# Holding back the residual transposes of two batches, and one DMA for both attention transposes of a step

## The chip, the cores and the metric

The kernel runs on one core of one Trainium2 chip. The metric is the device time of a whole execution in microseconds (us). Four engines compute on the core: TensorE (PE, with its weight loads shown as PEld), VectorE (DVE), ScalarE (ACT) and GpSimd (POOL). SyncE (SP) computes nothing here; it issues DMAs. POOL issues DMAs too, beside small copies. Sixteen DMA engines move the data of all of them.

## The reference

Eight batches, twelve heads, 448 tokens, head size 64. An attention with a squared ReLU in place of the softmax is followed by an MLP mixer: one pair of products over the tokens, one over the channels, each with a residual.

```python
scores = scale * np.matmul(q, k.transpose(0, 1, 3, 2))
attn = np.maximum(scores, 0.0) ** 2 / S
x = np.matmul(attn, v)            # then [B, S, H * D] = [8, 448, 768]

xt = x.transpose(0, 2, 1)
h = np.maximum(xt @ w_tok1, 0.0) @ w_tok2      # 448 -> 256 -> 448
u = x + h.transpose(0, 2, 1)
h2 = np.maximum(u @ w_ch1, 0.0) @ w_ch2        # 768 -> 1536 -> 768
return u + h2
```

Inputs and output are float32; the loads cast to bfloat16.

## The kernel before

**Tiling.** A step `i` takes four heads of one batch, so a batch has `DB` = 3 steps and the kernel `ND` = 24. In a step, `scores(i, c)` makes the score tiles for seven chunks of 64 keys (PE, L165), ACT applies the ReLU (L174), DVE squares (L181), `values` multiplies by V (PE, L193), and `values_out` writes the scaled result, channels on the partitions, into `xT` (L211). `xT` has one slot for even and one for odd batches, with 512 columns for the 448 tokens and zeros behind them.

**Token mixing.** The first product over the tokens needs the tokens on the partitions. `x_back` makes that transpose into `x_sb`: for the first `XDMA` = 8 steps with PE and a copy (L237, L246), from step index 8 on with DMA transposes issued by SP, one for each of the step's two blocks of 128 channels (L229). `token1` (L255) and `token2` (L278) are the two products; the addition at L286 writes `uT`, the mixed activations with channels on the partitions, for two batches in one tile (`uT_tiles`).

**Channel mixing.** `channel1` (L323) and `channel2` (L362) are the products over the channels. The second gives tokens on the partitions, so its residual must be turned as well: `u_back` issues on SP two DMA transposes a step from `uT` into `u_sb` (L311), six for a batch, 384 columns wide in even batches and 512 in odd ones, so that a pair of batches makes seven chunks of 128 tokens. L369 adds `u_sb` to the product, half a chunk at a time, and after the second half L381 stores the chunk with two DMAs on SP.

**Order.** The schedule is manual: each engine runs its instructions in the order in which the program emits them, and waits are derived from the tiles that they read and write. Loop index `i` from 4 on does `values(i - 1)`, `x_back(i - 1)`, `token1(i - 1)` and `token2(i - 1)`; by the index of the loop, step 7 holds `token2(6)`, step 8 `x_back(7)`, and step 9 `x_back(8)`, the first with DMA transposes. Between them `fill` takes units of channel mixing from `queue`, so that PE always has work; `channel_work(b)` puts a batch's units there, and the `channel2` units of batch 0 wait in `later` until those of batch 1 are queued. `channel2` runs for the first time in step 8.

**When residuals are turned.** `token2` calls `u_back` at once for the first two batches (L294, L295). For the others it leaves the step in `u_later`, which the main loop empties after `x_back` of the next index (L538, L539).

**POOL's queue.** Loads of Q, K and V (`load_four`) and of the weights go through POOL. `load_four(i + PRE)`, three steps ahead, is emitted once in each step; from index 9 on a one-element copy (`gate`, L542) stands before it that reads the last transposed `x_sb`, so that loads start only after it has landed. The last large weight load, the second half of `wc2`, is issued in step 5 (at 65 us).

**Buffers.** `x_sb`, `uT` and `r2` have two slots, `u_sb` and the output tile three, the raw Q, K and V tiles four. PSUM: two slots for scores, one for each of the two accumulators, two for the products (`bank`).

Of the kernel before, what the change touches and what calls it, by code (L numbers as in the profile page):

```python
# [10 lines left out]
BF16 = mybir.dt.bfloat16  # L11
# [5 lines left out]
def kernel(  # L17
# [11 lines left out]
    nc = tc.nc  # L29
# [6 lines left out]
    NP = H // 2  # L36
    ND = B * H // 4
    DB = H // 4
# [6 lines left out]
    NT = 2 * S // 128  # L45
# [7 lines left out]
    mix = ctx.enter_context(tc.tile_pool(name="mix", bufs=2))  # L53
# [8 lines left out]
    xT = [consts.tile([128, NP, SP], BF16, name=f"xT{i}") for i in range(2)]  # L62
# [115 lines left out]
    def square(keep=0):  # L178
        while len(squares) > keep:
            at = squares.pop(0)  # L180
            nc.vector.tensor_tensor(out=at, in0=at, in1=at, op=ALU.mult)  # L181
# [38 lines left out]
    x_tiles, r1_tiles, uT_tiles = {}, {}, {}  # L220
    XDMA = 8

    def x_back(i, place="bank", copy=None):
        b, d = divmod(i, DB)
        x_sb = mix.tile([128, 2, 4, 128], BF16, name="x_sb")
        x_tiles[i] = x_sb
        if i >= XDMA:
            for r in range(2):
                nc.sync.dma_start_transpose(  # L229
                    out=x_sb[:, r], in_=xT[b % 2][:, 2 * d + r, :]  # L230
                )
            return
        pool = ps_mm if place == "bank" else ps_acc
        ps = pool.tile([128, 2, 512], BF16, tag=place, name="x_ps")
        for r in range(2):
            for c in range(4):
                nc.tensor.matmul(  # L237
                    ps[:, r, c * 128 : (c + 1) * 128],
                    lhsT=xT[b % 2][:, 2 * d + r, c * 128 : (c + 1) * 128],
                    rhs=ident,  # L240
                    is_transpose=True,
                    start=True,
                    stop=True,
                    skip_group_check=True,
                )
        (copy or nc.vector.tensor_copy)(  # L246
            x_sb.rearrange("n r c d -> n (r c d)"), ps.rearrange("n r t -> n (r t)")
        )
# [17 lines left out]
    def token2(i, early=False, rs=(0, 1)):  # L266
        b, d = divmod(i, DB)
        if d == 0 and b % 2 == 0 and 0 in rs:
            uT_tiles[b // 2] = mix.tile([128, NP, 2 * S], BF16, name="uT_sb")
        r1 = r1_tiles[i]  # L270
        off = (b % 2) * S
        if early:
            parts = {r: ps_mm.tile([128, 512], FP32, tag="bank", name="h_ps1") for r in rs}
        else:
            parts = {r: ps_acc.tile([128, 512], FP32, tag=f"acc{r}", name="h_ps") for r in rs}
        for r in rs:
            for j in range(JC):
                nc.tensor.matmul(  # L278
                    parts[r][:, :S],
                    lhsT=r1[:, j, r * 128 : (r + 1) * 128],  # L280
                    rhs=wt2[:, j, :],
                    start=(j == 0),
                    stop=(j == JC - 1),
                )
        for r in rs:
            nc.vector.tensor_tensor(  # L286
                out=uT_tiles[b // 2][:, 2 * d + r, off : off + S],
                in0=parts[r][:, :S],
                in1=xT[b % 2][:, 2 * d + r, :S],
                op=ALU.add,  # L290
            )
        if 1 in rs:
            u_later.append(i)
            if i < 2 * DB:  # L294
                u_back(u_later.pop())  # L295


    r2_tiles, u_tiles, out_tiles = {}, {}, {}
    u_later = []

    def chunks(b):
        half = NT // 2
        return range(half) if b % 2 == 0 else range(half, NT)

    def u_back(i):
        b, d = divmod(i, DB)
        t = chunks(b)
        if d == 0:
            u_tiles[b] = mix.tile([128, NP, NT - NT // 2, 128], BF16, name="u_sb", bufs=3)
        for p in (2 * d, 2 * d + 1):  # L310
            nc.sync.dma_start_transpose(  # L311
                out=u_tiles[b][:, p, : len(t), :],
                in_=uT_tiles[b // 2][:, p, t.start * 128 : t.stop * 128],
            )

    def channel1(b, e):
        if b % 2 == 0 and e == 0 and b > 0:
            r2_tiles[b // 2] = mix.tile([128, EC, 2 * S], BF16, name="r2_sb")
        uT, r2 = uT_tiles[b // 2], r2_tiles[b // 2]
        off = (b % 2) * S  # L320
        ps = ps_mm.tile([128, 512], FP32, tag="bank", name="m1_ps")
        for g in range(CC):
            nc.tensor.matmul(  # L323
                ps[:, :S],
                lhsT=wc1[:, g, e * 128 : (e + 1) * 128],
                rhs=uT[:, g, off : off + S],
                start=(g == 0),
                stop=(g == CC - 1),
            )
        nc.scalar.activation(r2[:, e, off : off + S], ps[:, :S], AF.Relu)  # L330
# [23 lines left out]
    def channel2(b, t, half):  # L354
        r2 = r2_tiles[b // 2]
        cols = slice(half * HN, (half + 1) * HN)
        if half == 0:
            out_tiles[b, t] = outp.tile([128, DM], FP32, name="out_sb")
        o = out_tiles[b, t]
        ps = ps_mm.tile([128, 512], FP32, tag="bank", name="m2_ps")  # L360
        for e in range(EC):
            nc.tensor.matmul(  # L362
                ps[:, :HN],
                lhsT=r2[:, e, t * 128 : (t + 1) * 128],
                rhs=wc2[:, e, cols],
                start=(e == 0),
                stop=(e == EC - 1),
            )
        nc.vector.tensor_tensor(  # L369
            out=o[:, cols].rearrange("n (g d) -> n g d", d=128),  # L370
            in0=ps[:, :HN].rearrange("n (g d) -> n g d", d=128),
            in1=u_tiles[b][:, half * (CC // 2) : (half + 1) * (CC // 2), t - chunks(b).start, :],
            op=ALU.add,
        )
        last = b == B - 1 and t == NT - 1
        if half == 1 or last:
            part = cols if last else slice(0, DM)
            (b0, c0), (b1, c1) = divmod(2 * t, QC), divmod(2 * t + 1, QC)
            rows = [out[2 * (b // 2) + n].rearrange("(p c) m -> c p m", c=QC) for n in range(2)]
            for k, (n, c) in enumerate(((b0, c0), (b1, c1))):  # L380
                (nc.scalar if last and k else nc.sync).dma_start(  # L381
                    out=rows[n][c, :, part], in_=o[64 * k : 64 * (k + 1), part]
                )
        if half == 1:
            out_tiles.pop((b, t))
# [5 lines left out]
    def channel_work(b):  # L391
        for e in range(2 if b == 0 else 0, EC):
            queue.append((C1, lambda e=e: channel1(b, e)))
        for t in chunks(b):
            for j in range(2):
                later.append((C2, lambda t=t, j=j: channel2(b, t, j)))
        if b > 0:
            queue.extend(later)
            later.clear()
# [90 lines left out]
    i = DB  # L490
# [31 lines left out]
    for i in range(DB + 1, ND + 2):  # L522
        slow = i <= 2 * DB
        if i == 2 * DB + 1:
            rate[0] = (EC * C1 + NT * C2) / DB
        if i < ND:
            scores(i, 0)
            scores(i, 1)
        if 0 <= i - 1 < ND:
            values(i - 1, range(QC))  # L530
            values_out(i - 1)
        if i < ND:
            scores(i, 2)
        if i - 1 < XDMA:
            fill(1 / 3, least=1)
        if 0 <= i - 1 < ND:
            x_back(i - 1)
        while u_later:  # L538
            u_back(u_later.pop(0))  # L539
        if i + PRE < ND:  # L540
            if i - 1 >= XDMA:
                nc.gpsimd.tensor_copy(gate, x_tiles[i - 1][:1, 1, 3, 127:])  # L542
            load_four(i + PRE)
        if i == 5:
            load_wc2(1, 2)
        square()
        if i - 1 >= XDMA:
            fill(1 / 3)
        if i < ND:
            scores(i, 3)  # L550
            scores(i, 4)
        if i + 1 < ND:
            transposes(i + 1)
        square()
        if not slow:
            fill(2 / 9)
        if 0 <= i - 1 < ND:
            token1(i - 1)
        fill(1 / 3 if slow else 1 / 9, least=1)
        if i < ND:  # L560
            scores(i, 5)
            scores(i, 6)
        if 0 <= i - 1 < ND:
            token2(i - 1)
            if (i - 1) % DB == DB - 1:
                channel_work((i - 1) // DB)
        square()
        fill(1 / 3, least=1 if slow else 0)
    while queue:
# [31 lines left out]
```

## Time and profile before

| | before |
|---|---|
| median of 4 runs | 380.24 us (379.65 to 380.87) |
| the profiled execution | 379.94 us |
| its span in the profile | 378.2 us |
| granted TensorE clock | 1.00 |
| L323, channel1 on PE | 115.6 us busy, x564 |
| L362, channel2 on PE | 115.2 us busy, x672 |
| u_sb transposes (L311, SP) | 48, 3.9 us from issue to landing (median) |
| x_sb transposes (L229, SP) | 32, 2.4 us |
| POOL's gate copy (L542) | 12, 211 ns each |
| software DMA queue (POOL's loads) | 24,416 packets, 21.47 MB, 40.2% of 16 engines |
| hardware DMA queue (SP's) | 45,072 packets, 20.76 MB, 26.1% |

In the profile a group's line names its source line, its engine and operation, and the tiles it writes and reads. Busy time of PE is modelled for pipelined matmuls, so a PE that is always busy is not one at its peak; but a gap in it is time in which it had nothing to start. "X <- Y" under waits means that X stood idle until Y was done. A DMA instruction on SP or POOL is only the issue; the landing is counted from the issue to the arrival of the data. SP's issuing instructions don't count as busy time.

### The profile page before, as it was taken

Reading aid. Unit: us, or ns where it says so; the run is one execution under the profiler, and the core shown is the slowest. Engines: PE = TensorE matmul, PEld = TensorE weight load, DVE = VectorE, ACT = ScalarE, POOL = GpSimd, SP = SyncE. Lnnn points to the kernel's source line nnn. Section 1 sums busy time; section 2 is a strip of 40 time slices with the busy share of each in tenths; the row PEclk is TensorE's granted clock in tenths of the full one; section 3 lists DMA queues with packets and bytes.
Section 4 is the critical chain, followed back from the end, with each engine's and each line's share of the span. In section 5 each row is a group of like instructions: output and inputs, shape, how many; then the busy total and the mean of one; then the engine's idle time right before and its main releaser. Section 6 shows DMA issues by size and latency. Waiting matters only on the chain.

```text
span 378.2 us, 10110 instructions
## 1 busy us (share of the span) xinstructions
PE 365.8 (97%) x4335; PEld 200.8 (53%) x4335; DVE 206.8 (55%) x371; ACT 213.5 (56%) x297; POOL 97.1 (26%) x174
## 2 busy tenths in 40 slices
PE   8878999999989999999999999999999999999995
PEld 3444455555555564565555555555555654555563
DVE  2886688864567665465555575465555664121021
ACT  4996888877434457745676347654676346412400
POOL 8974544451030321430321303303300000000000
PEclk9999999999999999999999999999999999999999
DMA  8899999996157866846835867729551353433023
GB/s 154 113 159 183 200 191 175 190 174 94 42 76 160 176 104 132 106 74 148 140 74 75 156 135 131 122 51 172 92 102 22 70 126 79 58 69 85 0 62 108
DMA packets 69838, 43.31 MB, mean 115 GB/s; under 512 B 43872, under 2 KB 66336, under 8 KB 69792
## 3 DMA queue, kind: packets, MB, share of 16 engines
q0 software_dynamic: 24416, 21.47, 40.2%
q1 hardware_dynamic: 45072, 20.76, 26.1%
q8 instruction: 34, 0.56, 0.6%
q10 hardware_dynamic: 304, 0.43, 0.4%
q14 instruction: 12, 0.10, 0.1%
HBM read 43.38 MB, written 11.01 MB: 144 GB/s over the span
## 4 chain that ended last, share of the span: by engine, by line
PE 88%; DVE 4%; ACT 4%; DMA 2%; issue 1%; SPq 0%; ACTq 0%
PE m_ps L362 28%; PE m_ps L323 27%; PE sc_ps L165 9%; PE acc_ps L193 8%; PE t_ps L255 6%; PE h_ps L278 5%; PE qkT_ps L141 3%; ACT at L174 3%; DMA x_sb<-xT 2%; DVE uT_sb L286 1%; DVE at L181 1%; PE warm_ps L425 1%; DVE xT L211 1%; PE m_ps L341 1%; PE x_ps L237 1%
## 5 line engine op out<-in xcount | busy, mean ns | idle before, releaser
L174 ACT ACTIVATE at<-sc_ps 128x896 bf16<-128x896 f32 x168 | 145.1, 920 | 59.5 <-PE sc_ps L165 59.2
L323 PE MATMUL m_ps<-uT_sb,wc 128*128 128x448 bf16 x564 | 115.6, 353 | 0.2 <-DVE uT_sb L286 0.2
L362 PE MATMUL m_ps<-wc,r_sb 128*128 128x384 bf16 x672 | 115.2, 326 | 0.0
L181 DVE TENSOR_TENSOR at<-at 128x896 bf16<-128x896 bf16 x168 | 97.5, 623 | 6.6 <-ACT at L174 6.6
L362 PEld LDWEIGHTS <-r_sb 128*128 128x128 bf16 x672 | 64.3, 98 | 45.8 <-issue 4.1
L330 ACT ACTIVATE r_sb<-m_ps 128x448 bf16<-128x448 f32 x94 | 51.2, 545 | 60.0 <-PE m_ps L323 59.7
L323 PEld LDWEIGHTS <-wc 128*128 128x128 bf16 x564 | 53.3, 98 | 49.8 <-issue 4.3
L369 DVE TENSOR_TENSOR out_sb<-m_ps,u_sb 128x384 f32<-128x384 f32 x56 | 31.1, 556 | 60.4 <-PE m_ps L362 59.5
L165 PE MATMUL sc_ps<-qkT 64*64 64x448 bf16 x672 | 52.7, 360 | 2.9 <-ACT at L174 2.3
L286 DVE TENSOR_TENSOR uT_sb<-h_ps,xT 128x448 bf16<-128x448 f32 x48 | 27.8, 620 | 40.1 <-PE h_ps L278 40.1
L211 DVE TENSOR_SCALAR xT<-acc_ps 128x448 bf16<-128x448 f32 x45 | 26.1, 620 | 34.9 <-PE acc_ps L193 34.9
L193 PE MATMUL acc_ps<-at,v_raw 64*64 64x448 bf16 x672 | 38.6, 350 | 0.0
L542 POOL COPY gate<-x_sb 1x1 bf16<-1x1 bf16 x12 | 2.5, 211 | 133.3 <-DMA x_sb<-xT 133.3
L83 POOL DMA_DIRECT2D q_raw<-in_q_dram x48 | 29.0, 612 | 22.4 <-DMA wc<-in_moe_w_ch_dram 17.1
L83 POOL DMA_DIRECT2D v_raw<-in_v_dram x48 | 29.4, 631 | 15.3 <-PE sc_ps L165 6.2
L165 PEld LDWEIGHTS <-qkT 64*64 64x64 bf16 x672 | 15.6, 105 | 30.8 <-issue 26.6
L155 DVE COPY qkT<-qkT_ps 128x896 bf16<-128x896 bf16 x39 | 22.6, 619 | 14.4 <-PE qkT_ps L141 14.4
L83 POOL DMA_DIRECT2D k_raw<-in_k_dram x46 | 27.9, 626 | 1.5 <-DMA q_raw<-in_q_dram 1.0
L255 PE MATMUL t_ps<-x_sb,wt 128*128 128x256 bf16 x192 | 24.9, 273 | 2.1 <-DMA x_sb<-xT 1.4
L193 PEld LDWEIGHTS <-v_raw 64*64 64x64 bf16 x672 | 20.2, 107 | 12.1 <-issue 0.8
L263 ACT ACTIVATE r_sb<-t_ps 128x512 bf16<-128x512 f32 x24 | 14.3, 598 | 20.6 <-PE t_ps L255 20.5
L278 PE MATMUL h_ps<-wt,r_sb 128*128 128x448 bf16 x96 | 22.5, 355 | 0.0
(38 smaller groups left out, 118.8 us busy)
## 6 DMA issues: line engine op xcount, KB each, us to landing
out_dram<-out_sb SPq DMA_DIRECT2D x54, 192.0 KB, 3.8
q_raw<-in_q_dram POOLq DMA_DIRECT2D x48, 112.0 KB, 4.3
v_raw<-in_v_dram POOLq DMA_DIRECT2D x48, 112.0 KB, 5.7
k_raw<-in_k_dram POOLq DMA_DIRECT2D x46, 112.0 KB, 5.4
wc<-in_moe_w_ch_dram POOLq DMA_DIRECT2D x4, 1152.0 KB, 11.9
u_sb<-uT_sb SPq DMA_TRANSPOSE x48, 3.9
x_sb<-xT SPq DMA_TRANSPOSE x32, 2.4
k_first<-in_k_dram SPq DMA_DIRECT2D x1, 224.0 KB, 3.5
```

The source lines that it names most:

```text
L83: eng.dma_start(out=dst[64 * r : 64 * (r + 1)].rearrange("p g c d -> p g (c d)"), in_=src[b, h0 : h0 + 2].rearrange("g (p c) d -> p g (c d ...
L165: nc.tensor.matmul(ps[64 * r : 64 * (r + 1), g, :S], lhsT=sb[h, r, 1, c * 64 : (c + 1) * 64], rhs=sb[h, r, 0, :], start=True, stop=True, s ...
L174: nc.scalar.activation(at, ps[:, :, :S], AF.Relu)
L181: nc.vector.tensor_tensor(out=at, in0=at, in1=at, op=ALU.mult)
L193: nc.tensor.matmul(ps[r][64 * g : 64 * (g + 1), :S], lhsT=v_raw[h, g, c, :], rhs=at[h, g, :], start=(c == 0), stop=(c == QC - 1), skip_gro ...
L255: nc.tensor.matmul(ps[:, j, :], lhsT=wt1[:, c, j * 128 : (j + 1) * 128], rhs=x_sb[:, :, c, :], start=(c == 0), stop=(c == 3),)
L278: nc.tensor.matmul(parts[r][:, :S], lhsT=r1[:, j, r * 128 : (r + 1) * 128], rhs=wt2[:, j, :], start=(j == 0), stop=(j == JC - 1),)
L286: nc.vector.tensor_tensor(out=uT_tiles[b // 2][:, 2 * d + r, off : off + S], in0=parts[r][:, :S], in1=xT[b % 2][:, 2 * d + r, :S], op=ALU.add,
L323: nc.tensor.matmul(ps[:, :S], lhsT=wc1[:, g, e * 128 : (e + 1) * 128], rhs=uT[:, g, off : off + S], start=(g == 0), stop=(g == CC - 1),)
L330: nc.scalar.activation(r2[:, e, off : off + S], ps[:, :S], AF.Relu)
L362: nc.tensor.matmul(ps[:, :HN], lhsT=r2[:, e, t * 128 : (t + 1) * 128], rhs=wc2[:, e, cols], start=(e == 0), stop=(e == EC - 1),)
L369: nc.vector.tensor_tensor(out=o[:, cols].rearrange("n (g d) -> n g d", d=128), in0=ps[:, :HN].rearrange("n (g d) -> n g d", d=128), in1=u_ ...
```

## The change

Three things differ.

1. In `x_back`, the two DMA transposes of a step become one: its input is both channel blocks side by side, 1,024 columns, its output the whole of `x_sb`.
2. `token2` no longer calls `u_back` for the first two batches; all steps go to `u_later`. At index 7 (`2 * DB + 1`), after `token2(6)`, `hold_back(0, ...)` allocates batch 0's `u_sb` tile and `u_back` runs for its three steps. From index 8 on the main loop empties `u_later` of the steps before `i - 1`; at index 8 `hold_back(1, ...)` comes first, and steps 3, 4, 5 and 6 follow. From index 9 on it is one step an index, as before.
3. `hold_back` is new. It has POOL copy one element into each of the six channel blocks of the new `u_sb` tile. The transposes overwrite these elements, so they wait for the copies; and the copies wait for what they read: for batch 0 an element of the `uT` tile that `token2(6)` writes, for batch 1 an element of `x_sb` of step 7. On POOL the copies for batch 1 stand before `load_four(11)`.

```diff
         if i >= XDMA:
-            for r in range(2):
-                nc.sync.dma_start_transpose(
-                    out=x_sb[:, r], in_=xT[b % 2][:, 2 * d + r, :]
-                )
+            nc.sync.dma_start_transpose(
+                out=x_sb.rearrange("n r c d -> n (r c) d"),
+                in_=xT[b % 2][:, 2 * d : 2 * d + 2, :].rearrange("n r t -> n (r t)"),
+            )
             return
...
         if 1 in rs:
             u_later.append(i)
-            if i < 2 * DB:
-                u_back(u_later.pop())
...
     def u_back(i):
         b, d = divmod(i, DB)
         t = chunks(b)
-        if d == 0:
+        if b not in u_tiles:
             u_tiles[b] = mix.tile([128, NP, NT - NT // 2, 128], BF16, name="u_sb", bufs=3)
...
+    def hold_back(b, src):
+
+        u_tiles[b] = mix.tile([128, NP, NT - NT // 2, 128], BF16, name="u_sb", bufs=3)
+        for p in range(NP):
+            nc.gpsimd.tensor_copy(u_tiles[b][:1, p, 0, :1], src)
...
         if 0 <= i - 1 < ND:
             x_back(i - 1)
-        while u_later:
-            u_back(u_later.pop(0))
+        if i > 2 * DB + 1:
+            if i == 2 * DB + 2:
+                hold_back(1, x_tiles[i - 1][:1, 0, 0, :1])
+            while u_later and u_later[0] < i - 1:
+                u_back(u_later.pop(0))
...
             token2(i - 1)
             if (i - 1) % DB == DB - 1:
                 channel_work((i - 1) // DB)
+            if i == 2 * DB + 1:
+                hold_back(0, uT_tiles[1][:1, 0, :1])
+                for _ in range(DB):
+                    u_back(u_later.pop(0))
```

## The prediction

> **What bounds the kernel now.** I read the page's busy row first, then busy time by stage, then who TensorE (PE) waits for, then the chain of waits around the two waits left, and last the DMA view of the first of them.
>
> The page: busy time by engine, DMA share in 40 slices of 9.5 us, and the landings of the transposes that the change touches.
> ```profile
> PE 365.8 (97%) x4335; PEld 200.8 (53%) x4335; DVE 206.8 (55%) x371; ACT 213.5 (56%) x297; POOL 97.1 (26%) x174
> ...
> DMA  8899999996157866846835867729551353433023
> ...
> q8 instruction: 34, 0.56, 0.6%
> ...
> u_sb<-uT_sb SPq DMA_TRANSPOSE x48, 3.9
> x_sb<-xT SPq DMA_TRANSPOSE x32, 2.4
> ```
> PE is the bound. The DMA engines are full until about 85 us (nine digits of 8 or 9), nearly idle from 85 to 113 (6, 1, 5), moderate after.
>
> Busy time by stage (first pair: stage and length).
> ```profile
> 20.00:44.00 24.00, 20.73 (x314) 10.22 (x304) 17.69 (x29) 19.26 (x27) 15.43 (x25) 1.00 1.18 177
> 44.00:64.00 20.00, 20.00 (x336) 11.36 (x332) 15.79 (x29) 17.34 (x25) 7.18 (x12) 1.00 1.24 185
> 64.00:95.00 31.00, 30.82 (x439) 17.12 (x432) 19.73 (x36) 23.53 (x34) 12.13 (x20) 1.00 1.11 154
> 95.00:125.00 30.00, 28.98 (x360) 16.53 (x359) 19.27 (x36) 13.34 (x16) 4.94 (x10) 1.00 0.50 92
> 125.00:325.00 200.00, 199.98 (x2323) 109.76 (x2322) 114.41 (x209) 115.54 (x161) 40.33 (x75) 1.00 0.59 108
> ```
> From 44 to 95 us, where DMA is fullest, PE lacks 0.18 us of 51. Full DMA engines cost PE nothing there.
>
> What PE waits for between 44 and 374 us, all of it:
> ```profile
> PE t_ps L255 <- DMA x_sb<-xT: 1.4, 2, 1.0
> PE m_ps L323 <- DVE uT_sb L286: 0.2, 1, 0.2
> ```
> Between 20 and 44 us it waits 3.3 us, for ACT and DVE (L174, L246, L211, L286), not for a DMA. So what a change of DMA traffic can win is the two x_sb waits: 1.0 us at 110 and 0.4 us at 328, 0.37% of the run.
>
> The chain at the first of them (start, length, what):
> ```profile
> 104.21 1.14 DVE xT L211 x2
> 105.34 0.82 DVE at L181 x2
> 106.16 4.15 DMA x_sb<-xT
> 110.31 0.14 issue
> 110.45 1.03 PE t_ps L255 x8
> ```
> The second transpose takes 4.15 us here against the usual 2.4. The DMA view of 104 to 112 us says why (GB/s in slices of 0.2 us):
> ```profile
> GB/s 0 0 0 0 0 0 0 0 0 0 111 228 210 107 0 0 92 182 205 189 26 0 0 5 9 9 9 12 12 175 216 88 1 0 0 106 223 154 9 22
> ...
> q8 instruction: 1, 0.02, 1.1%
> ```
> The data of the first transpose goes at 106.0 to 106.8, of the second at 107.2 to 108.2. Then there are 1.2 us at 5 to 12 GB/s: one engine of the 16 delivers its share late. One instruction packet took 1.1% of 16 engines over 8 us, that is 1.4 us, on one engine. The wait at 328 looks alike (one q8 packet between 324.5 and 326.3).
>
> [...] from 29 to 34 us, with both queues full, q0 moved 815 packets and q1 750.[...]
>
> **The change part by part.**
>
> *Early transposes taken away.* Twelve u_sb transposes leave 25 to 75 us. PE waits for no DMA there, so POOL's loads come sooner into buffers that nobody lacks: k_raw's 0.4 us wait (PE's weight load at 40.2) lies behind L341, which ends at 40.30 in the chain. Gain 0; at most those 0.4.
>
> *Batch 0 in step 7.* hold_back(0) waits for the first half of token2(6)'s addition (L286 at 83.33, 1.16 for two: done 83.9). Its six POOL copies cost what L542's gate copy does, 0.2 us, so the first transpose can go at about 84.2. An issue takes SP 1.25 us, so the third starts at 86.7 and the sixth at 90.5; with 2.4 to 3.9 us from issue to landing they are in by 90.6 and 94.4. The first L369 that adds them starts at 96.30 and needs three; the second, at 99.05, the rest. Margin 4.6 us or more, cost 0; the worst case is a rival below. Behind the copies on POOL stand load_four(11)'s six loads, and they also stand behind hold_back(1), which waits for x_sb of step 7 (L246 at 91.95, done 92.64). They move from 81.3-90.4 to about 94-97.5; with 5.7 us of landing they are in by 103.2, and their first reader, transposes(11), comes near 123. Cost 0.
>
> *Batch 1 in step 8.* On SP eight transposes follow in a row (steps 3 to 5, and 6, which before went at 84): 93.0 + 8 x 1.25 = 103.0. Behind them wait the two stores of the first output tile (ready 99.6, 0.58 us each): 104.2. Then comes x_sb of step 8, whose input is ready at 104.19 + 1.16 = 105.35. So SP has 1.2 us to spare, and it is late if the eight average over 1.4 us. In the crowded early stage issues took 1.19 to 1.67, and up to 2.5 beside an instruction fetch. Six loads share the DMA engines there. I take +0.1; bounds 0 and +3.
>
> *Two x_sb transposes in one.* SP saves one issue in 16 steps. No row shows a 1,024-column transpose. A 384-column u_sb takes 1.25 us to issue (195 us) and a 512-column one 1.26 (166 us), so the cost is nearly fixed: I take 1.3, bounds 1.2 and 2.4 (two as one). Data starts when the issue ends (106.0 after 104.88 + 1.19). Before: ready 0.58 us sooner for the first half, two issues, then 0.6 us of data. Now: one issue after both halves, then 1.2 us. That is 0.58 + 1.3 + 1.2 = 3.1 against 2.5 + 0.6 = 3.1: equal. With 2.4 it is 1.1 later. In steps 10 to 20 PE comes to L255 1.7 to 2.5 us after the gate copy that marks the landing, so nothing is felt; only in steps 12 and 17, where a fetch meets the data too, is it 0.5 us (gate at 154.27, L255 at 154.74). In step 9: data at 105.4 + 1.3 = 106.7, fetch at 107.2 for 1.4 us, so that engine has 40% done and 60% of twice 1.0 us (its pace alone, 108.6 to 109.6) left after 108.7: 109.9, plus 0.75 to PE as before: 110.6 against 110.45. +0.15; bounds -1.0 (the fetch misses it) and +1.2. At 328 the same gives about +0.3, but PE also loses 16 semaphore instructions at L255,[...]: I take -0.2; bounds -0.4 and +0.6.
>
> *Waits.* SP gains waits for POOL, POOL for DVE; PE, ACT and DVE keep their order, PE loses 16 instructions that ran ahead of the matmuls.
>
> Sum: 0 + 0 + 0.1 + 0.15 - 0.2 = +0.05 us on the profiled execution (379.94 us; span 378.2 and 1.7 around it). That execution lies 0.3 below the median, 380.24; on the median it gives 380.3.
>
> **The rivals.**
> - *SP's queue becomes the wait of step 9 (slower).* Eight transposes and two stores stand before x_sb(8). For: they share the engines with six loads[...], so data may back up to the stores and to x_sb behind them. Against: PE's fetches are about 11 us apart, so one or two of the eight meet one. At 1.7 us each: 93 + 13.6 + 1.2 = 107.8, 2.4 late; so 382.3. It decides from 1.4 us each.
> - *The wide transpose costs two issues.* 1.1 us later everywhere: the waits at 110 and 328 grow by some 0.7 each, and steps 12 and 17, with 0.5 us to spare, wait 0.3 each: 382.2. For: twice the packets. Against: 384 to 512 columns cost 0.01 us.
> - *Both waits vanish.* The fetches fall clear of the data: 380.24 - 1.4 = 378.8. Against: at 110 PE's program before the fetch is unchanged, and the data still spans it.
> - *Batch 0's residual comes too late* for L369 at 96.3; DVE stands, PSUM stays full: +2, 382.2. Margins speak against it.
> - That the hold does nothing cannot be: the copies write the slots that the transposes overwrite.
>
> **How the numbers follow.** A change of 0.3% is 1.1 us, about what this kernel's measurement tells from none. Chances: no change to speak of (forecast) 0.58, SP's queue 0.18, both waits vanish 0.11, wide issue 0.09, late residual 0.04. The forecast gives 0.52 within 0.3%, 0.04 slower, 0.02 faster; the queue 0.15 slower, 0.03 within; vanishing waits 0.08 faster, 0.03 within; wide issue 0.06 and 0.03; late residual 0.03 and 0.01. Faster 0.10, within 0.62, slower 0.28. The range runs from 379.2 (one wait gone, with the runs' spread) to 382.1 (most of the queue's case).
>
> **What would show it.** Right: PE still full from 44 to 95 and 125 to 325 us; DMA digits lower before 85 and higher from 85 to 104; x_sb issues of 1.2 to 1.4 us; waits at L255 of about 1 and 0.3 us. Wrong: x_sb of step 9 issued after 106, waits of DVE at L369 for u_sb, x_sb issues of 2 us, or a PE busy time that differs from 365.8 by over 0.5 us.

## The result and the profile after

The changed kernel takes 380.39 us (median of 35 runs), the kernel before 379.83 (56 runs): a ratio of 1.0017, 95% interval 1.0004 to 1.0031. That is 0.1 us above the forecast and within the 0.3% that was called no change. The interval leaves out 1, so the change is a small loss rather than nothing. Ratios and counts of kept runs leave out, as slow, each run over 1.5% above the fastest of its kernel. The profiled execution took 380.32 us, 0.38 more than the one of before.

The page of the changed kernel: busy time, DMA share in 40 slices, landings.
```profile
PE 365.5 (97%) x4335; PEld 200.7 (53%) x4335; DVE 206.4 (55%) x371; ACT 213.5 (56%) x297; POOL 100.5 (27%) x186
...
DMA  8999999913998866847745797638451344433023
...
u_sb<-uT_sb SPq DMA_TRANSPOSE x48, 2.8
x_sb<-xT SPq DMA_TRANSPOSE x16, 3.3
```
PE's busy time differs by 0.3 us. The DMA gap of before, the slices 6, 1, 5 from 85 us on, has closed, and there is one from about 76 to 95 us (1, 3): the loads are through earlier. Batch 0's six transposes take little of 85 to 95; batch 1's eight and the six loads beside them fill 95 to 105.

Busy time by stage (start:end, length, then PE, PEld, DVE, ACT and POOL, granted clock, DMA share, GB/s):
```profile
44.00:64.00 20.00, 20.00 (x336) 11.37 (x332) 15.77 (x29) 17.34 (x25) 10.36 (x17) 1.00 1.19 195
64.00:95.00 31.00, 30.82 (x439) 17.12 (x432) 19.77 (x36) 23.51 (x34) 8.67 (x21) 1.00 0.55 93
95.00:125.00 30.00, 28.21 (x355) 16.06 (x354) 18.64 (x35) 12.71 (x16) 7.58 (x15) 1.00 0.95 146
```
From 64 to 95 us the DMA share halves, and PE's time is the same to the hundredth: the freed DMA engines bought nothing there. From 95 to 125 PE loses 0.77 us.

What PE waits for between 44 and 374 us, all of it:
```profile
PE t_ps L255 <- DMA x_sb<-xT: 1.8, 1, 1.8
PE m_ps L327 <- DVE uT_sb L286: 0.2, 1, 0.2
```
The two waits at L255, 1.0 and 0.4 us, have become one of 1.8, in step 9. The one near 328 us is gone. 1.8 - 1.4 is the 0.4 us by which the two profiled executions differ. The view leaves out waits under 0.15 us; there is one of 0.13 at L255 in step 17.

The chain of waits of step 9 (L385 is the store that was L381, L228 the wide transpose):
```profile
104.19 1.15 DVE xT L211 x2
105.33 0.21 SPq L385
105.54 0.05 issue
105.60 0.59 SPq L385
106.18 0.04 issue
106.23 0.03 SPq L228
106.26 0.03 issue
106.29 4.87 DMA x_sb<-xT
111.16 0.05 issue
111.20 1.05 PE t_ps L255 x8
```
SP is still issuing the two stores when x_sb's input is ready at 105.33, so the transpose starts 0.96 us late; then it takes 4.87 us. The DMA view of 104 to 112 us, in slices of 0.2:
```profile
GB/s 258 218 287 220 292 267 228 122 0 0 15 246 230 200 215 92 400 353 222 115 205 274 105 19 0 3 8 9 10 9 234 289 273 288 121 211 184 13 0 0
...
q8 instruction: 1, 0.02, 0.7%
```
Before, nothing moved from 104.0 to 106.0. Now residual transposes are still moving until 105.6 and the stores until about 108, and behind the instruction packet (0.7% of 16 engines over 8 us, that is 0.9 us) the tail stands again, at 3 to 10 GB/s from 109.0 us on.

### The profile page after: what moved, and what is told of

Read it like the earlier page. It is cut to its first block, busy times and chain, and to the rows that moved or that the text cites. A ratio compares the mean times of both kernels' runs of the same rounds, so it can differ in the third digit from the quotient of the medians.

```text
span 378.5 us, 10082 instructions
## 1 busy us (share of the span) xinstructions
PE 365.5 (97%) x4335; PEld 200.7 (53%) x4335; DVE 206.4 (55%) x371; ACT 213.5 (56%) x297; POOL 100.5 (27%) x186
## 4 chain that ended last, share of the span: by engine, by line
PE 86%; DVE 4%; DMA 4%; ACT 4%; issue 1%; POOL 0%; SPq 0%; POOLq 0%; ACTq 0%
PE m_ps L327 28%; PE m_ps L366 27%; PE sc_ps L165 9%; PE acc_ps L193 8%; PE t_ps L255 6%; PE h_ps L278 5%; DMA x_sb<-xT 3%; ACT at L174 3%; PE qkT_ps L141 2%; DVE uT_sb L286 1%; DMA q_raw<-in_q_dram 1%; DVE at L181 1%; DVE xT L211 1%; PE m_ps L345 1%; PE x_ps L237 1%
## 5 line engine op out<-in xcount | busy, mean ns | idle before, releaser
L366 PE MATMUL m_ps<-wc,r_sb 128*128 128x384 bf16 x672 | 115.2, 326 | 0.0
L366 PEld LDWEIGHTS <-r_sb 128*128 128x128 bf16 x672 | 64.3, 98 | 45.6 <-issue 3.9
L165 PE MATMUL sc_ps<-qkT 64*64 64x448 bf16 x672 | 52.7, 360 | 2.9 <-ACT at L174 2.3
L286 DVE TENSOR_TENSOR uT_sb<-h_ps,xT 128x448 bf16<-128x448 f32 x48 | 27.8, 620 | 39.4 <-PE h_ps L278 39.4
L165 PEld LDWEIGHTS <-qkT 64*64 64x64 bf16 x672 | 15.6, 105 | 30.8 <-issue 26.6
L255 PE MATMUL t_ps<-x_sb,wt 128*128 128x256 bf16 x192 | 25.0, 273 | 2.6 <-DMA x_sb<-xT 1.8
L255 PEld LDWEIGHTS <-wt 128*128 128x128 bf16 x192 | 18.2, 98 | 8.4 <-DMA x_sb<-xT 2.7
```

Of the source, the lines that this page charges most:

```text
L165: nc.tensor.matmul(ps[64 * r : 64 * (r + 1), g, :S], lhsT=sb[h, r, 1, c * 64 : (c + 1) * 64], rhs=sb[h, r, 0, :], start=True, stop=True, s ...
L255: nc.tensor.matmul(ps[:, j, :], lhsT=wt1[:, c, j * 128 : (j + 1) * 128], rhs=x_sb[:, :, c, :], start=(c == 0), stop=(c == 3),)
L286: nc.vector.tensor_tensor(out=uT_tiles[b // 2][:, 2 * d + r, off : off + S], in0=parts[r][:, :S], in1=xT[b % 2][:, 2 * d + r, :S], op=ALU.add,
L366: nc.tensor.matmul(ps[:, :HN], lhsT=r2[:, e, t * 128 : (t + 1) * 128], rhs=wc2[:, e, cols], start=(e == 0), stop=(e == EC - 1),)
```

## The experiments

Medians, and ratios to the kernel before run beside them (there its medians were 379.87 to 379.96 us; the first row is the one beside the changed kernel); the last column is what PE waits at L255 for the x_sb transposes in the profile.

| kernel | median us | ratio, 95% interval | waits at L255, us |
|---|---|---|---|
| before | 379.83 | | 1.0 + 0.4 |
| changed | 380.39 | 1.0017 (1.0004 to 1.0031) | 1.8 |
| hold only | 380.21 | 1.0014 (0.9999 to 1.0029) | 1.8 |
| wide transpose only | 379.44 | 0.9988 (0.9966 to 1.0010) | 1.0 + 0.2 |
| before, instruction packets shifted | 378.63 | 0.9995 (0.9963 to 1.0027) | none |
| changed, packets shifted | 382.44 | 1.0063 (1.0041 to 1.0085) | 2.9 |
| changed, step 6 later | 379.35 | 0.9968 (0.9950 to 0.9985) | 1.0 |
| before, unit ahead | 378.73 | 0.9959 (0.9934 to 0.9985) | none |
| changed, unit ahead | 379.11 | 0.9968 (0.9951 to 0.9985) | none |
| wide only, unit ahead | 379.22 | 0.9977 (0.9957 to 0.9996) | 0.2 |
| before, wc1 in quarters | 379.81 | 0.9992 (0.9978 to 1.0006) | 1.8 (two waits) |
| changed, step 6 later, unit ahead | 378.96 | 0.9973 (0.9963 to 0.9983) | none |
| hold, two x_sb transposes, step 6 later, unit ahead | 378.69 | 0.9958 (0.9942 to 0.9975) | none |
| before, quarters, unit ahead | 378.81 | 0.9970 (0.9956 to 0.9984) | none |

**Which half costs.** The changed kernel with the old loop of two transposes in `x_back`; and the kernel before with the wide transpose.
```diff
# hold only: from the changed kernel
-            nc.sync.dma_start_transpose(
-                out=x_sb.rearrange("n r c d -> n (r c) d"),
...
+            for r in range(2):
+                nc.sync.dma_start_transpose(
+                    out=x_sb[:, r], in_=xT[b % 2][:, 2 * d + r, :]
+                )
```


> The held residual transposes alone; each step keeps its two x_sb transposes. Theory (SP's queue): the eight transposes and two stores in front make x_sb of step 9 start about 1 us late, so the wait at L255 there is 1.8 us or more, and the wait near 328 us stays at 0.4: 0.8 us or more over before, some 380.7 against 379.9. Rival (the wide transpose is what costs): waits as before, 1.0 and 0.4 us, the same time as before within 0.3 us.

> One wide x_sb transpose a step alone; the residual transposes stay early. Theory: SP is free at step 9, x_sb is issued by 105.5 us, the wait there is 0.6 to 1.2 us and the one near 328 us is gone: 0 to 0.6 us under before. Rival (the wide transpose costs): the wait at step 9 is 1.5 us or more, 0.4 us or more over before.

The hold alone costs 0.34 us of median, less than the 0.8 expected and with an interval that just holds 1 (0.9999), and has the 1.8 us wait in step 9. That the wait near 328 us would stay did not come true: there is none in its profile. The wide transpose alone wins 0.4 us of median, with an interval that holds 1; it is not what costs. Its wait in step 9 is 1.0, the one near 328 is gone, and 0.2 us have come up in step 17. SP in the profile with the hold only, from 92 to 112 us (start, length, what; x9 is one transpose of batch 0 and the eight of step 8):
```profile
91.60 12.62 SPq L309 DMA_TRANSPOSE u_sb<-uT_sb  x9
104.32 1.18 SPq L385 DMA_DIRECT2D out_dram<-out_sb  x2
105.60 2.82 SPq L229 DMA_TRANSPOSE x_sb<-xT  x2
```
Against this the kernel with the wide transpose only, from 100 to 116 us:
```profile
103.99 1.16 DVE L211 TENSOR_SCALAR xT<-acc_ps 128x448 bf16<-128x448 f32 x2 [1.27 <-PE acc_ps L193]
...
105.21 1.23 SPq L228 DMA_TRANSPOSE x_sb<-xT  x1
```
Here SP is free and starts 0.06 us after its input is done.

**Two fewer in the queue.** The changed kernel, with step 6's two residual transposes behind x_sb of step 9.
```diff
-            while u_later and u_later[0] < i - 1:
+            while u_later and u_later[0] < (6 if i == 2 * DB + 2 else i - 1):
                 u_back(u_later.pop(0))
```


> The changed kernel, but the two residual transposes of step 6 are issued after x_sb of step 9 instead of before it (six transposes in a row in step 8 instead of eight). Theory (SP's queue and what is in flight in it delay x_sb of step 9): x_sb is issued near 105.4 us, its wait at L255 falls from 1.8 to 0.3 to 1.1 us, the time by 0.6 to 1.5 us, and the runs near 382.4 us get rare. Rival (the place in SP's queue does not matter, the instruction packet alone makes the wait): 1.5 us or more stay.

x_sb is issued at 105.56 instead of 106.29, the wait falls from 1.8 to 1.0 us, the time by 1.0 us, and none of 22 runs is near 382.4 us. So 0.8 us of the wait were the place in the queue. It is the start that the queue moved, not what follows: x_sb lands 4.93 us after its issue here, 4.95 with the wide transpose alone, where SP is free, and 4.87 in the changed kernel. The 1.0 that is left shows the tail again, in the DMA view of that kernel from 104 to 112 us:
```profile
GB/s 132 255 289 205 288 344 353 492 292 445 246 0 0 27 216 220 211 210 205 182 78 188 262 54 0 0 5 142 41 9 9 13 280 24 0 0 99 224 159 10
...
q8 instruction: 1, 0.02, 0.8%
```

**Is the tail the instruction packet?** Both profiles, before and changed, have 34 instruction packets (q8) for PE's 8,670 matmuls and weight loads, one for 255 on average. So 76 weight loads and 76 matmuls more at the start should make the packets fall elsewhere in what follows, and they move no other work. The matmuls of `keep_clock`, whose product is never used, are cut in three.
```diff
-                nc.tensor.matmul(
-                    warm_ps[h, :], lhsT=warm[h, :64], rhs=warm[h, :],
...
+                for lo, hi in ((0, 171), (171, 342), (342, 512)):
+                    nc.tensor.matmul(
+                        warm_ps[h, lo:hi], lhsT=warm[h, :64], rhs=warm[h, lo:hi],
```


> The kernel before with each of the 38 clock-keeping matmuls of the start cut into three pieces of the same total width: 76 more weight loads and 76 more matmuls on PE, [...]nothing else moves. The product of these matmuls is never used. Theory (an instruction packet on one DMA engine makes the two late landings): in steps 9 and 24, and in 12 and 17, the packet no longer falls into the data of x_sb; the waits of PE at L255 go from 1.4 us to under 0.4, the slack of steps 12 and 17 from 0.5 to about 2 us, and the time falls by 0.8 to 1.4 us. Rival (the landing is slow for another reason at these places: SP's queue, the end of an idle DMA stretch): both waits stay, and the time is that of before or up to 0.5 us more for the added instructions.

> The changed kernel with the same cut of the clock-keeping matmuls. Theory: of the 1.8 us wait at step 9 the part of the instruction packet goes and the part of SP's queue (x_sb issued near 106.3 instead of 105.4) stays: 0.2 to 0.6 us are left, the time is 1.0 to 1.6 us under the changed kernel's. If SP's queue made all of the wait, 1.5 us or more stay and the time does not fall.

On the kernel before the theory held in the profile: both waits are gone, and the slack of steps 12 and 17 is 2.3 and 1.6 us (gate copies at 151.00 and 224.72, L255 at 153.32 and 226.34) where it was 0.5. Its DMA view of 104 to 112 us has no slow tail behind the two transposes:
```profile
GB/s 0 0 0 0 0 0 0 0 0 22 209 223 183 20 0 0 105 229 209 112 2 0 10 188 214 79 1 0 82 77 169 179 90 85 38 58 54 15 45 202
```
Eight of its 13 kept runs lie at 377.9 to 378.9, some 1.5 us under before; but five took 381.2 to 382.5, four of them with a mean granted clock of 0.994, so the ratio's interval holds 1. No profile caught one of those five; what happened in them stays open (the section on the hold has a candidate).

The landings of whole traces say the same. In the kernel before, the x_sb transposes with no instruction packet in their data landed 2.4 to 2.7 us after the issue (20 landings), those with one 4.0 to 4.7 us (four). With the wide transpose, in the changed kernel, it is 3.2 to 3.3 us (seven) against 4.9 and 5.2 (two).

On the changed kernel the expectation failed: the time rose by 2 us. The packet now falls at 109.6 us, and there it meets the data of x_sb, issued as late as before the shift (106.26 us): it lands 5.81 us after the issue. So this run does not part the packet from the queue; the kernel with two fewer in the queue does. The DMA view of 104 to 112 us and, by single microseconds, the stages behind it (clock third from the end):
```profile
GB/s 6 8 8 10 12 171 22 58 289 287 236 274 224 428 246 323 169 123 338 323 200 182 175 173 93 64 108 282 342 72 8 0 4 8 9 10 87 296 196 214
```
```profile
112.00:113.00 1.00, 0.89 (x9) 0.80 (x10) 0.00 (x0) 0.00 (x0) 0.82 (x3) 1.00 0.27 60
113.00:114.00 1.00, 1.00 (x6) 0.54 (x4) 0.00 (x0) 0.60 (x1) 1.00 (x2) 0.57 0.80 163
114.00:115.00 1.00, 1.00 (x5) 0.45 (x3) 0.00 (x0) 0.00 (x0) 1.00 (x3) 0.50 0.99 140
115.00:116.00 1.00, 1.00 (x4) 0.45 (x3) 0.00 (x0) 0.00 (x0) 0.91 (x2) 0.50 1.00 209
116.00:117.00 1.00, 1.00 (x11) 0.29 (x9) 0.17 (x1) 0.00 (x0) 0.00 (x0) 0.72 1.17 171
```
The wait itself, until about 112.1, is 2.9 us. One microsecond later the granted clock falls: rows of 0.57, 0.50, 0.50 and 0.72 have lost 0.43 + 0.50 + 0.50 + 0.28 = 1.7 us of full-speed time, which at the 0.50 of the middle rows makes some 3.4 us. So the wait costs another 1.7 us: the 12 matmuls of L366 behind L255 take 3.63 us in place of 1.95. L255 itself starts 0.9 us later than in the changed kernel (112.11 against 111.20); the two profiled executions differ by 2.3 us in all. A wait of 2.9 us was followed by this fall, the one of 1.8 us in the changed kernel was not, in one profiled execution each.

This also reads the spread of the changed kernel's own runs. Nine of the 36 took 382.1 to 382.7 us, and only these have a mean granted clock of 0.993 to 0.996 where the rest have 0.998 to 1.000; the hold alone has three of 22 such. 1.7 us of 378 lost is 0.0045. None of these was profiled, so that they are waits of step 9 grown until the clock falls is an inference. Step 6 later, and the kernels below, bear it out: they differ from the changed kernel only from step 8 on, and have no such run.

**Work ahead of the wait.** In loop indices 9 and 24 one unit of channel mixing is taken ahead of token1; PE's work is the same in another order.
```diff
         if not slow:
             fill(2 / 9)
+        if i in (9, 24):
+            cost, unit = queue.pop(0)
+            credit[0] -= cost
+            unit()
```


> The kernel before with one unit of channel mixing moved ahead of token1 in loop indices 9 and 24 (12 matmuls of L362, 6 of L323), so that PE comes to L255 some 2 and 1.1 us later there. If the two waits at L255 are all that DMA costs this kernel, they vanish and the time falls by 1.0 to 1.5 us, to 378.4 or so; if work moved ahead only comes back as a wait later (at L278 or L286), it falls by less than 0.5.

> The changed kernel with the same units moved ahead. Theory (what the change costs is the wait of step 9, and the runs near 382.4 us are those where that wait grows and TensorE's clock falls): the wait is under 0.3 us, the time falls by 1.5 to 2.2 us, to 378.2 to 378.9, as fast as the kernel before with the same move, and runs 2 us above the rest get rare. Rival (the change costs something else too): 0.5 us or more slower than the kernel before with the same move.

> The wide x_sb transpose alone, residual transposes early, with the same units moved ahead. No wait of PE at L255 is left; 378.0 to 378.6 us, within 0.3 us of the kernel before with the same move, since the wide transpose won only where PE waited.

The kernel before gains 1.2 us, the changed one 1.3, and neither waits at L255. Nothing came back at L278 or L286, but in all kernels with the unit ahead PE now waits 0.4 us at L165 for ACT, near 116 us. In the changed kernel x_sb of step 9 is in time with nothing to spare: it lands at 111.19 us, and L255 starts at 111.24.

The changed kernel fell by less than the 1.5 expected and stays 0.4 us behind, between "as fast" and "0.5 or more". With the wide transpose alone it is 0.5, so that expectation failed, in the time and in the wait that was left. So with the waits covered the wide transpose is a small loss. Some 0.2 us of it is a wait in step 17. There a packet meets x_sb's data in both kernels (223.3 to 224.5 us with two transposes, 223.8 to 225.5 with the wide one); the two are in at 226.1 us, the wide one only at 227.0, after PE has come to L255. The rest was not traced. With the unit ahead no run of the changed kernel (of 22) is above 380.2: the group near 382.4 is gone with the wait.

**Both mendings, with and without the wide transpose.**

> The changed kernel with both mendings: step 6's residual transposes after x_sb of step 9, and one unit of channel mixing ahead of token1 in loop indices 9 and 24. Theory: no wait at L255 in steps 9 and 24 with 0.5 us or more to spare, 378.6 to 379.1 us, no run above 381. If the place in the queue still mattered with the unit ahead, it would be 0.3 us or more faster than with the unit alone (379.1).

> As the run before, with two x_sb transposes a step in place of the wide one. With the unit ahead, the kernel with early transposes was 0.4 us faster with two than with the wide one, where a wait of 0.2 us in step 17 had come up. Theory (the wide transpose is worth nothing once PE has work, and only moves the instruction boundaries): 378.4 to 379.1, within 0.4 us of the run with the wide one, no run above 381.

The second is the fastest tried by its ratio, level with the kernel before with the unit ahead: 378.69 us, 0.42% under the kernel before (0.25% to 0.58%) and 0.45% under the changed one by the medians; all its runs lie between 378.4 and 379.1. The step-6 move adds 0.15 us once a unit is ahead, less than 0.3: it gives x_sb of step 9 0.8 us to spare (110.44 us, L255 at 111.28), but its place in the queue no longer matters much when nobody waits.

**What the hold is good for.** The kernels with early residual transposes have another group of long runs, 381.1 to 384.7 us: 25 of the 177 runs of the kernel before that the comparisons with these experiments keep, from 2 of 27 to 13 of 69 in one comparison. With the hold and step 9 mended there is none in 73 (four kernels). In the profiles, wc1's second half lands 11.9 us after its issue at 38.05 in the kernel before, 2 us ahead of its first reader at 51.9; with the hold 9.7 us after 36.07, 6 us ahead. In the kernel before with shifted packets, where five of 13 runs were long, it lands at 51.37 us, 0.4 us ahead. To test whether this margin makes the long runs, its load was cut in two.
```diff
-            load_wc1(1, 2)
+            load_wc1(2, 4)
+            load_wc1(3, 4)
```


> The kernel before with the second half of wc1 loaded as two quarters, in the same place and with the same bytes, so that what channel1 needs at 52 us lands some 3 us sooner (it lands at 50 us in the profile of before). Some runs of the kernels with early residual transposes take 2 to 5 us more, those with the hold hardly any. Theory (in these runs the DMA engines are slower, wc1's second half is late for its first reader, PE waits and its clock falls): the runs above 382 us, about one in six before, get rare (0 or 1 of 22), the median stays within 0.3 us. Rival (another early load or wait makes these runs, or they have nothing to do with the loads): they stay at one in six.

> The kernel before with wc1's second half in two quarters and one unit of channel mixing ahead of token1 in loop indices 9 and 24; residual transposes early, two x_sb transposes a step. Theory (the long runs of the kernels with early transposes come from wc1's second half landing too close to its first reader): no or one run above 381 where the same kernel without the quarters had five of 22, and a median of 378.4 to 379.0. Rival (only the hold takes the long runs away): three or more runs above 381.

With quarters the first of them lands near 47.2 us, and none of 35 kept runs in the two kernels is above 381, with the residual transposes as early as ever. Of the kernel before, run beside these two, 6 of 61 kept runs are, so three or four were to be expected. One run more of the second kernel took 385.1 us; of all runs that is one of 36, against 10 of 65. (The last expectation gives the same kernel without the quarters five of 22 above 381; it had four.) So the counts speak for the weights' margin, and the hold isn't the only way to it. Two things stay open. The quarters also move a later load (the first half of `wc2` is issued at 47.52 us in place of 43.80), and no long run was caught in a profile, so the wait itself is not shown.

## Why the prediction was right, point by point

The number came out and the bound was read rightly, but one of the prediction's own signs of being wrong came true: x_sb of step 9 was issued after 106 us (106.29). The waits at L255 were 1.8 us and none, not about 1 and 0.3. The price came from the first rival's mechanism, at a small part of its size.

- *PE bound, no gain from freeing the DMA engines early: right.* From 44 to 95 us PE's time is unchanged, although the DMA share halves from 64 us on (1.11 to 0.55). What the prediction didn't see, since one profile can't show it, is the group of long runs that goes with a crowded early stage.
- *Batch 0 in time: right.* POOL's copies began at 84.00, the six transposes were issued from 84.2 to 92.9, and DVE shows no wait for u_sb.
- *SP's queue in step 8: the term that was mis-sized.* Taken as +0.1, with 1.25 us an issue and 1.2 us to spare. Measured: the eight took from 93.2 to 104.9, 1.46 us each, past the 1.4 at which the rival decides. Of that 1.37 is the issue (from 1.21 to 1.99, the longest beside an instruction packet) and 0.09 the pause between two issues, which the sum left out. The stores behind them ran until 106.2. The queue's part of the wait is 0.8 us (1.8 against 1.0 with two fewer). The rival's mechanism was there, at a third of its price of 2.4. In one run in four something of its full size came, if the runs of low clock are read as above. (The rival's 382.3 stands on the profiled execution; on the median, where the other rivals stand, it is 382.6.) SP from 92 us on, where x9 is the last transpose of batch 0 and the eight:
```profile
91.65 13.26 SPq L309 DMA_TRANSPOSE u_sb<-uT_sb  x9
```
- *The wide transpose: right in its issue.* One took 1.23 us (1.3 taken, bounds 1.2 and 2.4). That steps 12 and 17 had enough to spare held for step 12; in step 17 PE waits 0.13 us in the changed kernel and 0.2 in the two kernels with the wide transpose alone.
- *Step 9's wait without the queue: right within its bounds.* Taken as 1.15 with the packet; the kernels with the wide transpose and a free SP have 1.0, as before.
- *The wait at 328 us: right in sign.* -0.2 taken, as the author's estimate; -0.4 measured. With the wide transpose the packet starts some 3.0 us after the issue of x_sb, behind its data. But the hold alone lost the wait too: there the packet starts 1.0 us after the second issue, as before, and takes 1.16 us where it took 1.53. That is the 0.4 us, in one execution each, so the wait of before may come and go by itself.
- *The sum:* +0.05 taken, +0.38 between the profiled executions (0.8 - 0.4), +0.56 between the medians. Measured less taken is +0.7 for the queue, -0.15 for the wide transpose in step 9 and -0.2 at 328 us: errors that went against each other, which is luck. The further 0.2 between the medians shows in no wait of the two profiles. The range and "no change" held because all that the change touches is worth 1 to 2 us.

## What to carry to other kernels

When PE is full, ask of a freed resource who was waiting for it; here nobody was, and the price was paid where the moved work landed: ahead of the one DMA that PE did wait for. Work that is put off should be spread behind such a DMA, not stacked before it. A unit of ready work ahead of the consumer won 1.3 us here, the better order of the DMAs 1.0. Look at the spread of the runs besides the median: a margin of 2 us, which the profile shows as no wait at all, may be too small in some runs; the counts here point to it, though no profile has shown it.

## What the runs showed of the hardware

- Transposes with an instruction packet in their data landed later: 4.0 to 4.7 us after the issue instead of 2.4 to 2.7 (512 columns, the kernel before), 4.9 and 5.2 instead of 3.2 to 3.3 (1,024 columns, the changed kernel). The tail in the kernel before is six slices of 0.2 us at 5 to 12 GB/s, 11 KB in all; a sixteenth of such a transpose is 8 KB, so that one of the 16 DMA engines delivers late is an estimate from these two figures. 76 pairs of PE instructions more at the start took away both waits of the kernel before in its profile.
- In one execution a wait of PE of 2.9 us was followed by rows at a granted clock of 0.57, 0.50, 0.50 and 0.72, some 3.4 us at 0.50 by estimate; waits of 1.8 us (changed kernel, hold only) left it at 1.00.
- The issue of a transpose cost SP nearly the same at 384, 512 and 1,024 columns: 1.25, 1.26 and 1.23 us with little else in the queue; eight in a row beside six loads took 1.37 on average.
